# Products that nobody reads, added to TensorE's queue in the first slots of an attention and expert kernel

## Chip, cores and metric

The kernel runs on one core of a Trainium2 chip. The metric is the device time of one execution in microseconds (us). Five engines work side by side, each in its own fixed order: TensorE (PE, with the weight loads PEld beside it), VectorE (DVE), ScalarE (ACT), GpSimd (POOL) and SyncE (SP), from whose queue all DMAs of this kernel are issued.

## What is computed

Eight batches, eight heads, 576 positions, head width 64. First an attention with a bias that is a difference of running sums, then, on its output, a mixture of four attention experts of which two count for each position:

```python
cum = np.cumsum(np.maximum(s, 0.0), axis=-1)
bias = -(cum[:, :, :, None] - cum[:, :, None, :])
scores = np.where(causal, -1e9, q @ k.T / 8 + np.minimum(bias, 0.0))
x = softmax(scores) @ v                       # heads side by side: 512 columns
...
logits = x @ w_gate                           # the best 2 of 4 experts, softmax over the two
y_e = softmax(causal((x @ wq[e]) @ (x @ wk[e]).T / 8)) @ (x @ wv[e]) @ wo[e]
out = sum over the chosen e of weight_e * y_e
```

## The kernel before

The work is cut into pairs of heads (or of experts), numbered n = 0, 1, 2 and so on. Four pairs make a batch of the first attention; the projections (`p...`) and the expert pairs of a batch are mixed into the pairs of the next one. For each pair TensorE makes bf16 products that give bounds for the row maxima (`maxima`, line 482, six banks `m0` to `m5`), VectorE reduces them (`M0` to `M5`, line 496) and joins two columns (`cb`, line 516), TensorE turns the column of maxima (`mt`, line 520), ScalarE copies it with the sign changed (`mA`), and two small DMAs lay it as a row beside q (`mq`, line 529). Then come the scores in fp32r, two products for each piece (lines 547 and 552, steps `s0` to `s6`; the second reads the row of maxima and the running sums), the exponentials on ScalarE (`E0` to `E6`, line 568), masks and column sums on GpSimd (`d0` to `d3`, lines 589 to 614), and the products with v in float32 (`v0` to `v7`, line 645, written to tiles `pvp`). What is lost in rounding q and k is made up by the `l` steps (lines 457 and 462, on VectorE, for pair 1 on GpSimd).

The order of all of it is written out by hand. `slot(n)` gives the named steps of one slot, and FILLING (the first slots), MIDDLE and DRAINING list `slot:step` in the order in which they are issued. A slot prepares ahead: slot n holds the scores of pair n, the products with v of pair n-1, the maxima of pairs n+1 (banks 3, 4, 5) and n+2 (banks 0, 1, 2). So the run begins with slots -2 and -1, where only the maxima of pairs 0 and 1 can be made. Each engine takes its instructions in that order and waits by itself for what they need.

The eight banks of the accumulation memory go round in a list: `take` pops the bank that was given back longest ago, in the order of the text, and `give` puts one at the end. Who takes a bank waits until its last reader is done.

Before the first maxima, VectorE fills constant rows of K2 and Q2 (lines 220 and 221), makes the running sums (lines 281 to 292), and two DMAs bring those of pair 0 to K2 (line 410). `WOH` (the high part of wo) is written by ScalarE from the weights' steps `w0` and `w1` of slot 6.

Of the kernel before, what the change touches and what calls it, by code (L numbers as in the profile page):

```python
# [8 lines left out]
F32 = mybir.dt.float32  # L9
F32R = mybir.dt.float32r  # L10
# [29 lines left out]
def pieces(kt, q0, q1):  # L40
# [4 lines left out]
    for ci, segs in enumerate(SCHUNKS):  # L45
# [59 lines left out]
)  # L105
MIDDLE = {
# [1055 lines left out]
```

## Time and profile before

| | us |
|---|---|
| three timed runs | 678.67, 679.19, 681.6 |
| their median | 679.19 |
| span of the profiled execution, from its first to its last instruction | 682.3 |
| PE busy in it | 652.6 (96%) |
| DVE, ACT, POOL busy in it | 553.7, 453.1, 445.2 |
| mean granted clock of TensorE in it | 0.990 |

The profiled execution has no time of its own beside its span. The span lies 3.1 us above the median of the timed runs and 0.7 above the longest of them. A row of the timeline gives the start and the duration in us, the engine, line and operation, the tiles written and read, the shape, how many instructions are merged in the row, and in brackets how long the engine was idle before it and what ended that. The granted clock of a stretch is 1.00 for 2.4 GHz and 0.50 for 1.2 GHz, and the record of it begins with a row at 44.66 us: a stretch before that reads 1.00 in the windows for want of a record.

### The profile page before, as it was taken

To read this page: it belongs to the slowest core of one execution; us is meant where nothing else is said; L and a number is where in the kernel's file an instruction comes from. 1 tells how busy PE (TensorE), PEld (TensorE's weight loads), DVE (VectorE), ACT (ScalarE), POOL (GpSimd) and SP (SyncE) were. 2 spreads that over 40 slices of the span, in tenths; PEclk is the share of its full clock that TensorE was granted. 3 is DMA by queue.
4 is the path that set the end of the run, shared out by engine and by line. 5 is a ranking of instruction groups with operands and counts; after the bars stand their busy time and mean duration, and the time that the engine had idled before them with its cause. 6 is when DMAs were issued, how large, how long until landed. Compare 5 with 4: busy or idle time off the path is not lost.

```text
span 682.3 us, 16339 instructions
## 1 busy us (share of the span) xinstructions
PE 652.6 (96%) x5816; PEld 537.6 (79%) x5816; DVE 553.7 (81%) x1480; ACT 453.1 (66%) x972; POOL 445.2 (65%) x608
## 2 busy tenths in 40 slices
PE   1898899999999999999999999999999999999997
PEld 1665588878988798878987888878987788889875
DVE  6778988897889878888888878897888988871974
ACT  6567877666667756766767766676667766566464
POOL 8676676675786678576775677766876776837120
PEclk9999999979999999999999999999999999999989
DMA  4435352262347534554436633565346543340413
GB/s 131 113 104 139 115 161 73 74 177 55 107 111 187 163 91 106 154 145 132 120 94 159 183 90 89 148 163 152 95 103 165 161 113 106 86 123 11 99 40 123
DMA packets 52158, 81.21 MB, mean 119 GB/s; under 512 B 18430, under 2 KB 26622, under 8 KB 52078
## 3 DMA queue, kind: packets, MB, share of 16 engines
q1 hardware_dynamic: 52078, 80.18, 43.6%
q8 instruction: 46, 0.75, 0.5%
q14 instruction: 34, 0.28, 0.2%
HBM read 44.55 MB, written 10.09 MB: 80 GB/s over the span
## 4 chain that ended last, share of the span: by engine, by line
PE 83%; DMA 4%; DVE 4%; POOL 3%; SPq 2%; issue 2%; ACT 2%; ACTq 0%; POOLq 0%; DVEq 0%
PE pvp L645 18%; PE pq L855 15%; PE s L547 10%; PE s L552 10%; PE mx L482 9%; PE pw L855 8%; PE po L855 6%; DMA k<-cum 3%; PE sm L696 3%; DVE mx L496 1%; PE mt L520 1%; PE po L829 1%; DMA rb<-rr 1%; POOL r L611 1%; DVE q L457 1%
## 5 line engine op out<-in xcount | busy, mean ns | idle before, releaser
L496 DVE CUSTOM_DVE_ANT_0 mx<-mx,mask 128x512 f32<-128x512 f32 (+5 forms) x480 | 217.2, 471 | 61.4 <-PE mx L482 41.4
L589 POOL TENSOR_SCALAR_AFFINE_SELECT p<-p 128x256 f32<-128x256 f32 (+1 forms) x240 | 122.0, 509 | 148.5 <-ACT p L568 145.2
L568 ACT ACTIVATE p<-s 128x512 f32<-128x512 f32 x288 | 159.6, 588 | 65.4 <-PE s L552 48.2
L547 PE MATMUL s<-q,k 128*128 128x320 f32 (+3 forms) x672 | 175.2, 291 | 4.0 <-DVE k L462 1.6
L552 PE MATMUL s<-q,k 97*128 97x320 f32 (+3 forms) x672 | 163.3, 288 | 1.0 <-DMA q<-mr 1.0
L547 PEld LDWEIGHTS s<-q,k 128*128 128x128 f32 (+1 forms) x672 | 126.7, 189 | 17.6 <-issue 5.8
L611 POOL TENSOR_TENSOR r<-r,p 128x640 f32<-128x640 f32 x92 | 128.9, 1401 | 7.7
L552 PEld LDWEIGHTS s<-q,k 97*128 97x128 f32 (+1 forms) x672 | 126.3, 189 | 3.1 <-DMA q<-mr 1.7
L482 PE MATMUL mx<-k,q 96*64 96x384 bf16 (+6 forms) x960 | 97.8, 307 | 14.1 <-DMA k<-p 11.1
L645 PE MATMUL pvp<-p,v 128*64 128x128 f32 (+4 forms) x1024 | 101.9, 341 | 0.4 <-ACT p L568 0.4
L457 DVE TENSOR_TENSOR q<-raw,q 64x576 fp32r<-64x576 f32 x94 | 84.0, 895 | 14.9 <-ACT q L422 12.4
L645 PEld LDWEIGHTS pvp<-p,v 128*64 128x64 f32 x1024 | 70.5, 139 | 21.2 <-issue 3.1
L462 DVE TENSOR_TENSOR k<-raw,k 64x576 fp32r<-64x576 f32 x94 | 82.3, 888 | 5.0 <-DMA k<-k 3.1
L482 PEld LDWEIGHTS <-q 96*64 96x64 bf16 x960 | 47.6, 114 | 47.3 <-issue 14.5
L855 PE MATMUL pq<-xh,wqkh 128*128 128x288 f32 x256 | 77.7, 303 | 0.0
L855 PE MATMUL pq<-xh,wqkl 128*128 128x288 f32 x256 | 75.5, 295 | 0.0
L855 PE MATMUL pq<-xl,wqkh 128*128 128x288 f32 x256 | 75.4, 294 | 0.0
L425 ACT ACTIVATE k<-raw 64x576 fp32r<-64x576 f32 x96 | 64.5, 681 | 4.0 <-DMA raw<-in_qk_dram 1.7
L496 DVE DVE_READ_ACCUMULATOR2_ANT mcol<- 128x1 f32 x480 | 65.7, 137 | 0.9
L422 ACT ACTIVATE q<-raw 64x576 fp32r<-64x576 f32 x96 | 63.9, 678 | 3.4 <-DMA raw<-in_qk_dram 2.7
L606 POOL TENSOR_TENSOR r<-p 128x256 f32<-128x256 f32 x46 | 40.5, 880 | 35.4 <-ACT p L568 35.4
L659 ACT ACTIVATE pv<-pvp 128x256 f32<-128x256 f32 (+1 forms) x92 | 36.1, 405 | 40.6 <-PE pvp L645 40.6
(120 smaller groups left out, 1172.0 us busy)
## 6 DMA issues: line engine op xcount, KB each, us to landing
raw<-in_qk_dram SPq DMA_DIRECT2D x30, 576.0 KB
rb<-rr SPq DMA_DIRECT2D x92, 144.0 KB
q<-q SPq DMA_DIRECT2D x45, 288.0 KB
k<-k SPq DMA_DIRECT2D x39, 288.0 KB
v<-in_vm_dram SPq DMA_DIRECT2D x32, 256.0 KB
out_dram<-o SPq DMA_DIRECT2D x32, 256.0 KB
q<-mr SPq DMA_DIRECT2D x96, 2.2 KB
raw<-in_qk_dram SPq DMA_DIRECT2D x4, 288.0 KB
```

Source lines behind the costliest of these rows:

```text
L425: nc.scalar.activation(k2[0:64, j], get_raw(n, j)[64:128], AF.Copy)
L457: eng.tensor_tensor(a[64:128, j], get_raw(n, j)[0:64], q2[0:64, j].bitcast(F32), op=OP.subtract)
L462: eng.tensor_tensor(c[0:64, j], get_raw(n, j)[64:128], c[64:128, j].bitcast(F32), op=OP.subtract)
L482: nc.tensor.matmul(t[64 * j : 64 * j + 64, c0 : c0 + k1 - k0], q2[0:RC, 64 * qt : 64 * qt + 64], k2[0:RC, k0:k1], start=True, stop=True,)
L496: nc.vector.tensor_tensor_reduce(t[:, c0 : c0 + w], t[:, c0 : c0 + w], mask[:, m0 : m0 + w], scale=1.0, scalar=NEG, op0=OP.add, op1=OP.max ...
L547: nc.tensor.matmul(t[0:nk, c0 : c0 + q1 - q0], K1[r1(n)][:, j, k0 : k0 + nk], Q1[r1(n)][:, j, q0:q1], start=True, stop=False,)
L552: nc.tensor.matmul(t[0:nk, c0 : c0 + q1 - q0], K2[r2(n)][0 : RM + 1, j, k0 : k0 + nk], Q2[r2(n)][0 : RM + 1, j, q0:q1], start=False, stop= ...
L568: nc.scalar.activation(ptile[n][:, x % 2, 512 * ci : 512 * ci + 512], tl[x], AF.Exp, scale=0.125)
L589: nc.gpsimd.affine_select(out=a, in_=a, pattern=[[0, 2], [1, nk]], compare_op=OP.is_ge, fill=0.0, base=0, channel_multiplier=-1,)
L611: add(r[:, :, q0:S], r[:, :, q0:S], p[:, :, 1024 + c : 1024 + c + S - q0], op=OP.add)
L645: nc.tensor.matmul(cur[h][64 * j : 64 * j + 64, q0 - PVC[h] : q1 - PVC[h]], vsl(j, kt), ptile[n][:, j, c : c + q1 - q0], start=first, stop ...
L855: nc.tensor.matmul(t[0:nk, 0:w], l, r, start=(x == 0), stop=(x == len(terms) - 1))
```

## The change

54 steps named `e`, `er`, `eq` and `ef` are put into FILLING; the order of all other steps stays as it was. Each takes one bank or two, multiplies a constant tile by itself into them on TensorE and gives them back at once. Nobody reads the result. The constant tile is the memory of `WOH`, whose first 256 float32 columns VectorE sets to 1.0, ahead of its other fills; read as bf16 they are 512 columns, every second one zero.

- `e`: one bf16 product, 128 rows by 128 columns of weights, 512 columns streamed.
- `er`: two bf16 products, each on one half of the rows (64 by 128), 512 columns each.
- `eq`: four bf16 products, each on a quarter of the array (64 by 64), 512 columns each.
- `ef`: two fp32r products on the halves of the rows (64 by 128), 256 columns each.

28 of them (13 `e`, 6 `er`, 6 `eq`, 3 `ef`) stand at the very start, 12 `e` after the last maxima of pair 0 are reduced, and 14 `e` at seven places further on.

```diff
 FILLING = (
+    "0:e 0:e 0:e 0:e 0:e 0:e 0:e 0:e 0:e 0:e 0:er 0:er 0:er 0:er 0:er 0:eq 0:eq 0:eq 0:eq 0:eq "
+    "0:ef 0:ef 0:ef 0:e 0:er 0:e 0:eq 0:e -2:h1 -2:h3 -2:h2 -2:h0 -2:hc -1:m5 -2:m1 -1:m4 -2:M1 "
...
+    "-1:lq -2:M0 0:e 0:e 0:e 0:e 0:e 0:e 0:e 0:e 0:e 0:e 0:e 0:e -1:mt -1:h3 0:h1 0:l1 0:l0 -1:hc "
...
+    "0:f2 0:hc 1:ld 0:lq 0:e 1:m5 0:d0 0:m0 0:s6 0:mt 0:E4 0:s5 0:mA 1:lk 1:l0 0:m1 0:m2 0:E2 1:m4 "
+    "0:E5 0:M1 1:h1 1:h3 1:M5 0:M0 0:E6 1:M4 0:e 0:e 1:m3 1:l1 1:lq 1:M3 1:h2 0:mq 1:hc 1:s4 1:s5 "
+    "1:s6 1:s1 1:s2 1:E6 1:E5 1:s3 1:cb 0:M2 1:E2 0:e 0:e 0:e 1:mt 1:w0 1:s0 0:d1 0:lv 0:d2 1:l3 "
+    "2:h2 2:hc 1:E4 1:h0 2:h3 0:e 1:m0 1:v2 1:l2 1:v4 1:v3 1:v5 1:mA 1:E1 1:E3 1:v0 1:E0 2:h0 2:h1 "
...
+    "2:E1 2:E3 3:m5 2:m2 1:V0 2:s5 3:m4 3:lk 1:M2 2:M5 2:cb 2:ld 0:e 2:mt 2:M2 2:mA 2:l1 2:m0 2:a0 "
...
+    "3:m2 3:V0 3:E6 3:s2 3:E2 3:E0 3:M0 3:r4 2:V0 2:V1 3:mq 4:m5 2:d3 0:e 4:v2 3:d0 4:s3 3:n1 3:E5 "
...
+    "4:l1 5:l2 5:w0 3:d3 4:a1 5:h0 4:A1 4:w0 5:h2 4:mq 4:v6 4:E1 4:hc 0:e 0:e 0:e 0:e 0:e 5:m4 "
...
     fill(0)
 
+    idle = const.tile([P, 2, DM], F32R, tag="woh", name="woh")
+    WOH = idle
+    nc.vector.memset(idle[:, 0, 0:256].bitcast(F32), 1.0)
     nc.vector.memset(K2[1][64:96].bitcast(F32), 0.0)
...
+    def spare(kind):
+
+        w = WOH[:, 0, 0:256].bitcast(BF16)
+        a = take("e0")
+        if kind == "e":
+            nc.tensor.matmul(a, w[:, 0:P], w, start=True, stop=True)
+            give(a)
+            return
+        c = take("e1")
+        for r, t in enumerate((a, c)):
+            k = slice(64 * r, 64 * r + 64)
+            if kind == "er":
+                nc.tensor.matmul(t, w[k, 0:P], w[k], start=True, stop=True)
+            elif kind == "ef":
+                nc.tensor.matmul(
+                    t[:, 0:256], WOH[k, 0, 0:P], WOH[k, 0, 0:256], start=True, stop=True
+                )
+            else:
+                for o in (0, 64):
+                    nc.tensor.matmul(t[o : o + 64], w[k, 0:64], w[k], start=True, stop=True)
+        give(a)
+        give(c)
...
     for n, x in order(pairs):
-        if x in steps[n]:
+        if x in ("e", "er", "eq", "ef"):
+            spare(x)
+        elif x in steps[n]:
             steps[n].pop(x)()
```

## Rows read from the trace of the kernel before

**Rows 1.** The page: the engines' busy time and share of the span, and the granted clock in 40 slices of the span (tenths).

```profile
PE 652.6 (96%) x5816; PEld 537.6 (79%) x5816; DVE 553.7 (81%) x1480; ACT 453.1 (66%) x972; POOL 445.2 (65%) x608
...
PEclk9999999979999999999999999999999999999989
```

**Rows 2.** Windows of the whole program: stretch, its length, busy time (and instructions) of PE, PEld, DVE, ACT and POOL, granted clock, share of the DMA engines, GB/s.

```profile
44.70:82.20 37.50, 32.87 (x303) 21.50 (x299) 34.04 (x88) 28.82 (x59) 25.36 (x34) 1.00 0.48 135
82.21:85.61 3.40, 3.40 (x20) 2.18 (x18) 3.16 (x14) 3.11 (x7) 3.15 (x7) 0.50 0.29 83
...
143.65:150.40 6.75, 6.63 (x44) 5.01 (x45) 5.66 (x13) 3.48 (x9) 4.39 (x7) 0.50 0.44 86
...
659.10:662.40 3.30, 3.30 (x22) 2.08 (x20) 2.48 (x4) 1.67 (x5) 1.52 (x5) 0.50 0.29 98
```

**Rows 3.** Timeline of PE: neighbouring score products in three stretches (the first of each two streams 320 columns, and the next starts when those have gone in), and two products of 512 columns near the end. The row at 25.65 holds two banks of maxima, each two products of 512 columns on the two halves of the array's columns.

```profile
22.16 0.47 PE L552 MATMUL s<-q,k 97*128 97x320 f32 x1
22.43 0.36 PE L547 MATMUL s<-q,k 128*128 128x192 f32 x1
...
25.65 1.06 PE L482 MATMUL mx<-k,q 96*64 96x512 bf16 x4
...
45.60 0.31 PE L552 MATMUL s<-q,k 97*128 97x320 f32 x1
45.75 0.25 PE L547 MATMUL s<-q,k 128*128 128x192 f32 x1
...
82.66 0.47 PE L552 MATMUL s<-q,k 97*128 97x320 f32 x1
82.93 0.36 PE L547 MATMUL s<-q,k 128*128 128x192 f32 x1
...
671.28 0.39 PE L829 MATMUL po<-woh,xh 128*128 128x512 f32 x1
671.51 0.39 PE L829 MATMUL po<-wol,xh 128*128 128x512 f32 x1
```

**Rows 4.** Windows of the first 60 us, columns as in rows 2: from the first reduction to the first score, the scores of pairs 0 and 1, the first products with v, and what follows.

```profile
12.45:21.60 9.15, 3.62 (x29) 1.96 (x25) 8.89 (x25) 4.12 (x7) 8.73 (x21) 1.00 0.27 78
21.76:37.90 16.14, 16.07 (x77) 12.98 (x77) 12.37 (x42) 8.60 (x17) 10.97 (x17) 1.00 0.46 132
37.90:44.66 6.76, 6.07 (x33) 3.68 (x35) 3.23 (x8) 5.39 (x11) 2.92 (x6) 1.00 0.34 83
44.66:60.00 15.34, 14.12 (x137) 9.92 (x133) 14.61 (x47) 11.49 (x23) 13.84 (x19) 1.00 0.42 118
```

**Rows 5.** Timeline of PE: the first maxima, the turn of pair 0, the maxima of pair 1, the first score, the first unbroken run of products with v, two later waits of PE, and the later of the products with v of pair 1.

```profile
10.69 0.37 PE L482 MATMUL mx<-k,q 96*64 96x256 bf16 x1 [10.69 <-DMA k<-p]
11.46 2.56 PE L482 MATMUL mx<-k,q 96*64 96x256 bf16 x19 [0.39 <-DMA k<-p]
18.10 0.37 PE L520 MATMUL mt<-ident,mcol 128*9 128x128 f32 x1 [4.08 <-DVE mcol L496]
18.40 1.76 PE L482 MATMUL mx<-k,q 96*64 96x320 bf16 x16
21.76 0.61 PE L547 MATMUL s<-q,k 128*128 128x320 f32 x1 [1.60 <-DVE k L462]
...
38.59 0.37 PE L520 MATMUL mt<-ident,mcol 128*9 128x128 f32 x1 [0.76 <-DVE mcol L496]
...
40.20 4.29 PE L645 MATMUL pvp<-p,v 128*64 128x320 f32 x20
...
51.27 0.56 PE L482 MATMUL mx<-k,q 96*64 96x256 bf16 x8 [0.54 <-DVE mcol L496]
...
55.13 1.68 PE L645 MATMUL pvp<-p,v 128*64 128x192 f32 x16
...
80.06 0.64 PE L482 MATMUL mx<-k,q 96*64 96x512 bf16 x4 [1.85 <-DMA k<-cum]
```

**Rows 6.** Timeline of DVE: two fills, the first reduction, the last of pair 0 and the last step ahead of the first score, and the three reductions at which it waited for PE.

```profile
1.11 1.02 DVE L220 MEMSET k<- 32x1152 f32 x1 [1.11 <-PEq L1150]
...
3.39 0.11 DVE L228 MEMSET ones<- 128x64 f32 x1
...
12.47 0.57 DVE L496 CUSTOM_DVE_ANT_0 mx<-mx,mask 128x384 f32<-128x384 f32 x1 [3.93 <-PE mx L482]
...
17.66 0.23 DVE L496 CUSTOM_DVE_ANT_0 mx<-mx,mask 128x64 f32<-128x64 f32 x1
...
20.86 0.75 DVE L462 TENSOR_TENSOR k<-raw,k 64x576 fp32r<-64x576 f32 x1
...
26.34 0.70 DVE L496 CUSTOM_DVE_ANT_0 mx<-mx,mask 128x512 f32<-128x512 f32 x1 [2.06 <-PE mx L482]
...
31.05 0.57 DVE L496 CUSTOM_DVE_ANT_0 mx<-mx,mask 128x384 f32<-128x384 f32 x1 [1.26 <-PE mx L482]
...
44.91 0.57 DVE L496 CUSTOM_DVE_ANT_0 mx<-mx,mask 128x384 f32<-128x384 f32 x1 [3.70 <-PE mx L482]
```

**Rows 7.** Timeline of POOL: where it begins on the masks and sums of pairs 0 and 1 after a wait, and its last step for pair 1.

```profile
26.98 0.41 POOL L589 TENSOR_SCALAR_AFFINE_SELECT p<-p 128x256 f32<-128x256 f32 x1 [3.80 <-ACT p L568]
...
42.02 0.73 POOL L606 TENSOR_TENSOR r<-p 128x256 f32<-128x256 f32 x1 [3.75 <-ACT p L568]
...
50.52 0.45 POOL L614 TENSOR_TENSOR r<-r,p 64x128 f32<-64x128 f32 x1
```

**Rows 8.** Timeline of SP, DMA issues: the running sums of pair 0 and its row of maxima (two DMAs each).

```profile
8.64 1.58 SPq L410 DMA_DIRECT2D k<-p  x2
...
18.80 1.53 SPq L529 DMA_DIRECT2D q<-mr  x2
```

More of the change, by code (lines that the diff above doesn't have):

```diff
@@ L242, in tile_attention_then_moe @@
     WVGL = const.tile([P, NC, 260], F32R, tag="wvgl", name="wvgl")
-    WOH = const.tile([P, 2, DM], F32R, tag="woh", name="woh")
     WOL = const.tile([P, 2, DM], F32R, tag="wol", name="wol")
```

72 rows, old and new, of the table FILLING are left out of this document.

## The prediction

> **What bounds the kernel now.** I read the page's first lines, then windows, then the engines' timelines of the first 60 us. On the page PE is busy for 96% of the span, and the granted clock is 90% or more in all but two of its 40 slices [rows 1]. That leaves nothing for added products to win, unless they change the clock, so the reader should look at where the clock is low. Of the windows from 44.70 us on, three read 0.50, in all 13.5 us: 82.21 to 85.61, 143.65 to 150.40, 659.10 to 662.40 [rows 2]. What the page hides is the start. No row tells the clock before 44.66; it has to be read from the products. A score product of 320 columns takes 0.27 us till the next starts at 22.16, and 0.15 at 45.60; in the stretch that is granted 0.50, at 82.66, it takes 0.27 again [rows 3]. So TensorE runs at 1.2 GHz from its first product to about 44.7 and at 2.4 after that.
>
> Who sets the pace in those 44.7 us? Three parts [rows 4]. Up to 21.6 it is VectorE: busy 8.89 of 9.15 us from its first reduction, at 12.47, to its last step ahead of the first score [rows 4, 6]; PE waits 4.08 us in there for the last maxima of pair 0 [rows 5]. From 21.76 to 37.90 it is PE: busy 16.07 of 16.14. From 37.90 to 44.66 again PE, with 6.07 of 6.76, most of it one run of products with v, 40.20 to 44.49 [rows 4, 5]. VectorE waits for PE's maxima in these two parts three times: 2.06, 1.26 and 3.70 us, 7.0 together [rows 6]; POOL waits 3.80 and 3.75 us for exponentials, which wait for scores [rows 7]. From 44.66 to 60 VectorE is busy 14.61 of 15.34 [rows 4]: a faster PE helps there only by what reaches it earlier.
>
> **The first 28 steps.** They remove nothing. The constant tile costs VectorE one fill ahead of its others: 256 columns, by the fill of 1152 in 1.02 us and that of 64 in 0.11 [rows 6] about 0.28 us. It pushes the two fills behind it, the running sums and so the DMA issued at 8.64 [rows 8], which the first maxima await (10.69 and 11.46, [rows 5]): +0.3 us there. The products can start at about 1.5. A product of 512 columns takes 0.23 us at the high level [rows 3] and by the 0.27 for 320 columns 0.43 at the low one. At the low level: 13 `e` 5.6 us; `er` and `eq` 12 x 0.43 = 5.2 if the parts of the array work beside each other; 3 `ef` 0.6. Sum 11.4. If the row halves go one after the other, 5.2 + 0.6 more, 17.2. That column halves go together is in the row at 25.65: four products of 512 columns in 1.06 us [rows 3]; of row halves the trace of before has none. I take 11.4, the nearest row.
>
> The Trainium skill, "TensorEngine Tiling (Array Packing)", section "Tiling Modes", says that tiles work independently and that row halves are such tiles. By it the sum is 11.4; no run here shows it.
>
> If the level rises half way, at about 6, the products end near 6 + (11.4 - 4.5)/2 = 9.5, inside PE's wait for the DMA (to 10.69), and cost nothing. If it never rises they end at 12.9, and the first maxima come up to 1.4 late; with 17.2 and a rise at 6 they end at 12.4, 0.7 after the second DMA with its 0.3. That is the price if the cover is gone.
>
> Does the level rise? What PE did before each rise: before 44.66 an unbroken run of float32 products with v on both column halves, all 128 rows [rows 5]. What did not raise it: 16 us of scores and maxima with PE busy throughout [rows 4], half of which fill 97 rows or 96 by 64. So being busy is not enough here, and the added products, all rows and all columns back to back, are nearer to the run that raised it than to the scores that didn't.
>
> The Trainium skill, "TensorE: Matmul & The Clock Gate", Part 1, has the low clock as the default that matmul activity lifts. By that alone the scores should have lifted it well before 44.66; the trace disagrees, with its 16.07 busy us at 0.27 per 320 columns.
>
> **The 12 steps after the last maxima of pair 0.** Each takes the oldest bank. Two are free at once, four come free as the reductions go on, so the products spread over PE's wait of 4.08 us. The sixth bank's reduction is the last, at 17.66 to 17.95 [rows 6]; behind it stand five products and only then the turn `mt`: 5 x 0.23 = 1.2 us at the high level, 2.2 at the low. Queued behind: `mt` (18.10), the copy, two DMAs (18.80), the maxima of pair 1 (18.40) [rows 5, 8]. VectorE reads the latter only after 21.6, so they have room. The row of maxima is needed at 22.16; its second DMA is issued at some 19.6 and, if it takes the 2.05 us from 8.64 to 10.69 [rows 5, 8], lands at 21.6: 0.5 to spare. The reductions gain some 0.3 from a faster first bank. So the first scores start 0 to 1.6 us later; I take 0.3.
>
> **What the high level gives from 21.76 on.** PE's work there halves, but the saving counts only until something else is late. On VectorE's side the three waits are the ceiling, 7.0 us. First wait: the four score banks ahead of the reduced one take 21.76 to 25.65 at the low level, 2 less at the high one: 1.8 of 2.06 comes back. Second: 0.9 of 1.26, since VectorE itself comes to it earlier. Third: the products with v go from 4.29 to 2.15: 2.1 of 3.70. Together 4.8. On POOL's side, its start moves with the exponentials and it works without a break from 42.02 to 50.97; if it starts 3.2 earlier it ends pair 1 at 47.8, and the later products with v of pair 1, at 55.13 before [rows 5, 7], would need it by 55.13 - 4.8 = 50.3. So POOL does not take it away; VectorE, busy 95% after 44.66 [rows 4], is next.
>
> **The other 14.** Six stand ahead of 40 us, in PE's waits for VectorE that a faster PE makes longer (0.76 at 38.59 already, [rows 5]): nothing at the high level. One follows just before the products with v, hidden by the same. Two in slot 2 and the end of slot 3 have no wait of their own in the rows: 2 x 0.23 = 0.5. The five in slot 4, 1.2 us, lie in the wait of 1.85 us for the running sums, from 78.2 to 80.06 [rows 5]. In the profiled execution the clock falls at 82.2 soon after that wait, and PE, all busy, loses half of 3.4 us, 1.7 [rows 2]. If the five prevent it, 0 to 1.7 comes back; the timed runs are 0.7 to 3.6 shorter than the profiled span, so I take 0.4, near the low end. The ring of banks: each added step hands the next real product a bank freed later. Bounds 0 and, for a few of them, the 0.54 that PE waits for a reduction at 51.27 [rows 5]: I take 0.3.
>
> **Sum.** -4.8 + 0.3 + 0.5 + 0.3 - 0.4 = -4.1 (the fill's 0.3 is within the later start). The timed runs carry no profile, so I set it against the median: 679.2 - 4.1 = 675.1. After 60 us each slot waits for the one before, so I let it reach the end whole.
>
> **Rivals.**
> *It falls back before the scores* (0.27). Between 13 and 21.7 PE has only the 12 products and 1.8 us of maxima; the falls in the profile came behind waits of PE (1.85 us before the fall at 82.2). If TensorE is at 1.2 GHz when the first score starts, the scores run as before, and every `e` stands in a PE that is busy throughout: seven at 0.43 less the 0.76 of wait is 2.2, the start is up to 1.6 late, the fill 0.3: +4.1, less up to 2.1 if the extra products bring the rise forward. 681.2 to 683.3, I say 682.1, slower. For it: the spread of the products, those 16 us that didn't lift the clock. Against: at the low level each `e` lasts twice as long and fills more of the wait. The point that decides is the spacing of the first scores.
> *Caught by another engine* (0.17). The level is high, but POOL or the DMAs for pairs 1 and 2 hold: only the first wait and a part of the second come back, 2.5, less 1.1: 677.5 to 678.
> *The constant tile doesn't lift the clock at all* (0.08): 12.9 to 18.7 for the end of the first 28, 1.5 to 7 late, and 2 to 4 for the others: 683 to 690.
> *More comes back* (0.05): all 7.0 of the waits and the 1.7: 671.
>
> **Chances and range.** The forecast, 672.5 to 676.8, has 0.43. Half a per cent, 3.4 us, is about what a measurement of this kernel can tell from no change: faster below 675.8, slower above 682.6. Faster: three quarters of the forecast and the last rival, 0.37. Slower: a quarter of the fall back and most of the dead tile, 0.14. The rest, 0.49, is within. The range takes in the forecast, the catch and most of the fall back: 672.0 to 682.5, with 0.15 or so outside.
>
> **What would show it.** Right: score products of 320 columns 0.15 apart at 22, VectorE's three waits shorter, the products with v of pair 0 over by about 39, the same row of pair 1 near 51, a first maxima no later than 11.5. Wrong: 0.27 apart at 22 with `e` products 0.43 apart between them; a first maxima after 12; the high level at 22 but POOL or a DMA as the releaser of the next slots.

## The result, and the profile after

| | us |
|---|---|
| after, median of 20 runs | 682.42 (675.87 to 686.88) |
| before, median of 20 runs on the same chip | 678.33 (674.71 to 682.54) |
| ratio, 95% interval | 1.0054, 1.0031 to 1.0078 |
| profiled execution of after: its time, its span | 683.88, 682.2 |

The change costs half a per cent, where the prediction had a gain of 4.1 us. The time lies at the upper end of the range, 0.1 under its bound, and at 682.1 a rival had been set; that rival's mechanism is not what happened, as the rows show. The ratio leaves out one slow execution of after (686.88), so it is not the quotient of the two medians.

The page of after: busy time of the engines, and the granted clock in 40 slices of the span.

```profile
PE 661.3 (97%) x5897; PEld 536.5 (79%) x5897; DVE 549.9 (81%) x1481; ACT 453.1 (66%) x972; POOL 450.1 (66%) x608
...
PEclk9889899999999999999999999999999999999999
```

Beside [rows 1] PE is 8.7 us longer busy, and the low slices now stand in the first 90 us. Windows of after, columns as in rows 2, cut where the granted clock changes:

```profile
6.59:16.82 10.23, 8.12 (x70) 3.28 (x67) 6.42 (x22) 6.51 (x11) 8.52 (x21) 1.00 0.31 93
16.83:20.23 3.40, 2.98 (x12) 1.13 (x13) 3.29 (x7) 1.36 (x4) 3.35 (x4) 0.50 0.00 0
20.24:30.47 10.23, 6.54 (x56) 4.63 (x52) 6.20 (x23) 3.76 (x8) 4.59 (x8) 1.00 0.60 161
30.48:40.71 10.23, 9.91 (x44) 6.95 (x44) 8.75 (x25) 7.24 (x15) 7.44 (x10) 0.50 0.18 59
...
81.68:88.50 6.82, 6.82 (x45) 4.76 (x45) 4.25 (x17) 4.77 (x9) 5.80 (x9) 0.50 0.50 140
```

So TensorE reaches 2.4 GHz at 6.59, falls to 1.2 at 16.83, is up again at 20.24, falls at 30.48 for 10.2 us and once more at 81.68. In the third row PE is busy only 6.54 of 10.23 us. The timeline of PE, with the rows that answer rows 3 and 5, says why (line 340 is `e`, 347 `er`, 354 `eq`, 349 `ef`; 509 the maxima, 547 the turn, 574 and 579 the scores, 672 the products with v):

```profile
1.26 4.45 PE L340 MATMUL e<-woh 128*128 128x512 bf16 x10 [1.26 <-DVE woh L224]
5.64 1.70 PE L347 MATMUL e<-woh 64*128 64x512 bf16 x10
7.27 1.27 PE L354 MATMUL e<-woh 64*64 64x512 bf16 x20
...
10.79 0.27 PE L509 MATMUL mx<-k,q 96*64 96x256 bf16 x1
11.46 1.45 PE L509 MATMUL mx<-k,q 96*64 96x256 bf16 x19 [0.40 <-DMA k<-p]
...
17.25 2.29 PE L340 MATMUL e<-woh 128*128 128x512 bf16 x5 [0.53 <-DVE mcol L523]
19.34 0.42 PE L547 MATMUL mt<-ident,mcol 128*9 128x128 f32 x1
...
21.95 0.41 PE L579 MATMUL s<-q,k 97*128 97x320 f32 x1 [0.57 <-DMA q<-mr]
...
23.32 0.31 PE L579 MATMUL s<-q,k 97*128 97x320 f32 x1
23.47 0.26 PE L574 MATMUL s<-q,k 128*128 128x192 f32 x1
...
29.03 0.56 PE L509 MATMUL mx<-k,q 96*64 96x256 bf16 x8 [3.01 <-DMA k<-cum]
...
29.77 0.28 PE L547 MATMUL mt<-ident,mcol 128*9 128x128 f32 x1
...
32.29 1.08 PE L340 MATMUL e<-woh 128*128 128x512 bf16 x2 [0.32 <-ACT p L595]
...
34.30 0.47 PE L579 MATMUL s<-q,k 97*128 97x320 f32 x1
34.56 0.36 PE L574 MATMUL s<-q,k 128*128 128x192 f32 x1
...
40.45 0.41 PE L547 MATMUL mt<-ident,mcol 128*9 128x128 f32 x1
...
41.77 2.24 PE L672 MATMUL pvp<-p,v 128*64 128x320 f32 x20
...
80.36 0.59 PE L340 MATMUL e<-woh 128*128 128x512 bf16 x2 [1.59 <-ACT p L595]
```

Four things are to be seen. The first maxima are where they were (10.79 and 11.46, against 10.69 and 11.46 in [rows 5]), so the prefix is hidden. The score product of 320 columns at 23.32 is followed after 0.15 us: the first scores do run at the high level, as forecast. Then stands a wait of 3.01 us for `k<-cum` that rows 5 do not have there: it is the load of pair 2's running sums. And the scores of pair 1 behind it are 0.26 us apart again (34.30), with two `e` ahead of them that last 1.08 us together.

Why are the sums late? The DMA issues of SP in after:

```profile
20.09 1.53 SPq L556 DMA_DIRECT2D q<-mr  x2
21.66 0.52 SPq L1138 DMA_DIRECT2D cum<-p  x1
...
25.62 0.28 SPq L440 DMA_DIRECT2D k<-cum  x1
```

In before, the issues of SP that follow the row of maxima of [rows 8] by one place and by three:

```profile
20.37 0.52 SPq L1111 DMA_DIRECT2D cum<-p  x1
...
24.34 0.28 SPq L413 DMA_DIRECT2D k<-cum  x1
```

SP issues in order. The row of maxima (`mq`) waits for the turn, 1.24 us later than before; behind `mq` stands the store of the running sums of all pairs to memory (`-1:cu`, line 1138), and behind that the load of pair 2's part (`0:hc`, line 440), which must wait until the store has landed. Everything slides by 1.3 us. The chain of work of after in this stretch (start, duration, what; the longest pieces) goes through exactly these:

```profile
17.25 2.29 PE e L340 x5
...
20.09 0.78 SPq L556
20.91 0.71 SPq L556
21.66 3.89 DMA cum<-p
25.62 3.28 DMA k<-cum
...
29.03 0.56 PE mx L509 x8
```

This stretch of it begins with the five `e` behind the last reduction. The same maxima in before:

```profile
27.85 0.90 PE L482 MATMUL mx<-k,q 96*64 96x256 bf16 x8
```

There a PE at the low level came to them at 27.85 without a wait; the sums, issued at 24.34, were there at about 27.6 if the load took the same 3.28 us (an estimate). A PE at the high level gets there at 26.0 and stands. On VectorE (timeline, the waits that answer rows 6):

```profile
24.72 0.70 DVE L523 CUSTOM_DVE_ANT_0 mx<-mx,mask 128x512 f32<-128x512 f32 x1 [1.22 <-PE mx L509]
...
29.80 0.75 DVE L484 TENSOR_TENSOR q<-raw,q 64x576 fp32r<-64x576 f32 x1 [2.64 <-PE s L574]
31.16 0.57 DVE L523 CUSTOM_DVE_ANT_0 mx<-mx,mask 128x384 f32<-128x384 f32 x1 [0.61 <-PE mx L509]
...
44.29 0.57 DVE L523 CUSTOM_DVE_ANT_0 mx<-mx,mask 128x384 f32<-128x384 f32 x1 [1.80 <-PE mx L509]
```

The three waits of rows 6 shrank from 7.02 to 3.63 us together, and a new one of 2.64 us took most of that.

### The profile page after: what moved, and what is told of

Same layout as the page of the kernel before. It is cut to its first block, busy times and chain, and to the rows that moved or that the text cites. A ratio compares the mean times of both kernels' runs of the same rounds, so it can differ in the third digit from the quotient of the medians.

```text
span 682.2 us, 16497 instructions
## 1 busy us (share of the span) xinstructions
PE 661.3 (97%) x5897; PEld 536.5 (79%) x5897; DVE 549.9 (81%) x1481; ACT 453.1 (66%) x972; POOL 450.1 (66%) x608
## 4 chain that ended last, share of the span: by engine, by line
PE 82%; DMA 6%; DVE 4%; ACT 3%; issue 2%; SPq 1%; POOL 1%; ACTq 0%; DVEq 0%; POOLq 0%
PE pvp L672 16%; PE pq L882 15%; PE s L574 10%; PE s L579 10%; PE mx L509 9%; PE pw L882 8%; PE po L882 7%; PE sm L723 3%; DVE mx L523 2%; DMA k<-cum 2%; DMA rb<-rr 1%; DMA q<-mr 1%; PE mt L547 1%; PE po L856 1%; ACT p L595 1%
## 5 line engine op out<-in xcount | busy, mean ns | idle before, releaser
L616 POOL TENSOR_SCALAR_AFFINE_SELECT p<-p 128x256 f32<-128x256 f32 (+1 forms) x240 | 124.4, 519 | 145.1 <-ACT p L595 141.0
L574 PE MATMUL s<-q,k 128*128 128x320 f32 (+3 forms) x672 | 172.8, 287 | 1.2 <-ACT k L452 0.7
L579 PE MATMUL s<-q,k 97*128 97x320 f32 (+3 forms) x672 | 161.3, 285 | 2.2 <-DMA q<-mr 2.2
L574 PEld LDWEIGHTS s<-q,k 128*128 128x128 f32 (+1 forms) x672 | 124.9, 186 | 14.2 <-issue 4.5
L579 PEld LDWEIGHTS s<-q,k 97*128 97x128 f32 (+1 forms) x672 | 124.0, 186 | 4.9 <-DMA q<-mr 3.4
L509 PE MATMUL mx<-k,q 96*64 96x384 bf16 (+6 forms) x960 | 95.2, 301 | 6.0 <-DMA k<-cum 4.8
L672 PE MATMUL pvp<-p,v 128*64 128x128 f32 (+4 forms) x1024 | 100.0, 336 | 0.1
L509 PEld LDWEIGHTS <-q 96*64 96x64 bf16 x960 | 46.0, 112 | 40.1 <-issue 15.9
```

What stands on the lines that cost most here:

```text
L509: nc.tensor.matmul(t[64 * j : 64 * j + 64, c0 : c0 + k1 - k0], q2[0:RC, 64 * qt : 64 * qt + 64], k2[0:RC, k0:k1], start=True, stop=True,)
L574: nc.tensor.matmul(t[0:nk, c0 : c0 + q1 - q0], K1[r1(n)][:, j, k0 : k0 + nk], Q1[r1(n)][:, j, q0:q1], start=True, stop=False,)
L579: nc.tensor.matmul(t[0:nk, c0 : c0 + q1 - q0], K2[r2(n)][0 : RM + 1, j, k0 : k0 + nk], Q2[r2(n)][0 : RM + 1, j, q0:q1], start=False, stop= ...
L616: nc.gpsimd.affine_select(out=a, in_=a, pattern=[[0, 2], [1, nk]], compare_op=OP.is_ge, fill=0.0, base=0, channel_multiplier=-1,)
L672: nc.tensor.matmul(cur[h][64 * j : 64 * j + 64, q0 - PVC[h] : q1 - PVC[h]], vsl(j, kt), ptile[n][:, j, c : c + q1 - q0], start=first, stop ...
```

## Experiments

Theories, by letter: A, the five products behind the last reduction hold the turn, and with it SP's queue with the store and the load of the sums; PE waits, and the clock falls behind that wait. B, the later products cost PE their own time, or the waits for banks. C, the first 28 (or their fill) delay the start. D, only how often the clock falls back in an execution counts, not the change. Ratios are to the kernel before, on the same chip in the same session, with 95% intervals. Diffs are against the changed kernel, most of them as what became of the lists of steps. A rise or fall is that of the one profiled execution.

**Parts alone.** The first 28 with the fill; the 12 without the others; the 14 without the others (each with the fill).

```diff
 only28:  the list keeps its first two lines
-"-1:lq -2:M0 0:e (x12) -1:mt"   and the 14
+"-1:lq -2:M0 -1:mt"
 only12:  keeps "0:e (x12)" alone;   only14:  keeps the 14 alone
```

> The constant tile and the first 28 steps alone; the 12 and the 14 are left out. Theory A (the five products behind the last reduction hold the turn of pair 0, and with it the store of the running sums that stands behind it in SP's queue): the turn is at 18.0 to 18.4, the load of the sums of pair 2 is issued near 24.3 as before, no 3 us wait of PE for it; the time is that of before, 676.5 to 679.5. Theory B (each later product costs PE its own time, where the clock is low or where it waits for a bank; the start plays no part): the time is that of before too, 677.5 to 679.5. Theory C (the first 28 and the fill themselves delay the start): first maxima over 0.5 us later than 10.69 and 11.46, and 680 or more.

> The constant tile and the 12 steps behind the last reduction of pair 0 alone. TensorE is then at 1.2 GHz when they run, unless they lift it. Theory A: the turn of pair 0 comes 2 us later than at 18.10, the store of the sums and the load behind it as well; 679.5 to 682. Theory B: 12 x 0.43 mostly in PE's wait, 678.5 to 680. Theory C: 678 to 679.

> The constant tile and the 14 later steps alone. Theory A: the turn of pair 0 at 18.1 as before, the time 678 to 680. Theory B: the seven ahead of 42 us cost 2 us at the low level, the five in slot 4 wait for banks that ScalarE holds and push the maxima behind them by 1 us: 681 to 683. Theory C: 678 to 679.

only28: 1.0012 (0.9984 to 1.0039). The first maxima come at 10.81 and 11.49, no wait for the sums, the turn at 17.39. The clock rises at 4.3 and falls at 14.5 until 24.8. So the 28 cost nothing that can be seen, and without the 12 the level is gone before the scores: C falls. only12: 1.0034 (1.0013 to 1.0055), the turn at 18.67, and the wait for the sums is there without the prefix: 2.79 us before 27.78, the clock low from 27.2. only14: 1.0017 (0.9986 to 1.0048), the clock rises at 37.1. Of the three parts only the 12 have an interval that lies above 1, as A says; the three intervals overlap.

**The store of the sums ahead of the row of maxima.** All 54 steps stay; only SP's order changes.

```diff
-"-1:lq -2:M0 0:e ..."   "... -1:m1 -1:cu 0:h2"
+"-1:cu -1:lq -2:M0 0:e ..."   "... -1:m1 0:h2"
```

> The changed kernel with one DMA moved: the store of the running sums (line 1138) stands ahead of the 12 steps in SP's queue and no longer behind the row of maxima of pair 0. Theory A: the store is issued near 14, the load of pair 2's sums no later than 24, PE's wait of 3.0 us at 26 goes and the scores of pair 1 start near 31 and not at 33.9; 678 to 680.5, 2 to 4 below the changed kernel. Theory B: the wait goes, the time stays within 1.5 of 682.4. Theory C: as theory B.

1.0003 (0.9977 to 1.003): the half per cent is gone. The store is issued at 12.15 instead of 21.66. But the load still goes out at 23.05, since a load of raw q and k (`0:ld`) stands ahead of it, and PE waits 2.18 us. Its clock falls at 26.3, for 10.2 us. From the issues of SP and the timeline of PE in cu_early:

```profile
23.05 0.29 SPq L440 DMA_DIRECT2D k<-cum  x1
...
27.24 0.90 PE L509 MATMUL mx<-k,q 96*64 96x256 bf16 x8 [2.18 <-DMA k<-cum]
```

So a part of A's chain is cut, not all. Two things follow. The load goes out 1.3 us earlier here than in before (24.34), and a PE at the high level waits for it all the same: the held turn is only a part of the wait of after, the earlier PE is the other. And the time is level although the wait and the fall behind it are still in this profile, which speaks against A as the whole of the half per cent.

**Fewer behind the last reduction, and the five of slot 4.** e12to7 keeps 7 of the 12, so none is left behind the last reduction; no_hc5 leaves out the five of slot 4.

```diff
 e12to7:
-"-1:lq -2:M0 0:e (x12) -1:mt"
+"-1:lq -2:M0 0:e (x7) -1:mt"
 no_hc5:
-"4:E1 4:hc 0:e 0:e 0:e 0:e 0:e 5:m4"
+"4:E1 4:hc 5:m4"
```

> The changed kernel with 7 of the 12 steps behind the last reduction of pair 0, so that none waits for the last bank. Theory A (five products behind the last reduction hold the turn and SP's queue behind it): the turn at 17.4 and not at 19.3, the load of pair 2's sums issued near 23.8 and not at 25.6, PE's wait of 3.0 us 1 to 2 shorter; time 678 to 680.5. Theory B (the later 14 cost, not the 12): within 1.5 of 682.4. Theory D (it is only how often the clock falls back, whatever the turn does): fewer products in the wait let it fall more often, 682 to 684.

> The changed kernel without the five steps in slot 4. They took five banks in the order of the ring and waited 1.59 us for ScalarE with the maxima of pair 6 behind them. Theory A: within 1 of 682.4, or 681.4 at the least. Theory B: those maxima start no later than the sums' load allows, 679.5 to 681.4. Theory D: a wait of PE is open again, 682 to 684.

e12to7: 1.0041 (1.0014 to 1.0069), the turn at 18.20, the wait for the sums 0.31 us, and the clock is low from 19.06 to 25.9, in the first scores. The chain of A is nearly gone and the ratio is hardly better than that of after, which speaks against A. That the five not only hold the turn but also keep TensorE up would explain it; it is not shown. no_hc5: 1.0097 (1.0065 to 1.013; six runs). The wait of 3.14 us is there, and the clock falls at 81.39 for 6.8 us as it does with the five. For these five B falls: in this profile they neither bring nor prevent that fall.

**The bank of an added step given back to the head of the list**, so that the next real product gets the bank that it had before the change.

```diff
+    def back(t):
+        banks.insert(0, taken.pop(id(t))[1])
-            give(a)
+            back(a)
...
-        give(a)
-        give(c)
+        back(c)
+        back(a)
```

> The changed kernel, but the banks of the added steps go back to the head of the ring, so that each added product takes the bank that the next real one takes and none waits for a reduction on its own account. Theory A: the 12 run in one go from 13 to 15.8, the turn is at 17.4, the five in slot 4 end before the sums' load lands: 677 to 680. Theory B: the bank waits go, the products' own time stays: 679.5 to 681.5. Theory D: PE then stands still from 15.8 to 17.4 and from 18.5 to 21; the clock falls back at the same rate, 681 to 683.

1.024 (1.0208 to 1.0272; six runs), the clearest slowdown of all. Each added product now goes into the bank of the one before. Timeline of PE:

```profile
1.26 6.37 PE L343 MATMUL e<-woh 128*128 128x512 bf16 x10 [1.26 <-DVE woh L224]
...
19.48 2.61 PE L512 MATMUL mx<-k,q 96*64 96x256 bf16 x20
...
22.69 6.98 PE L343 MATMUL e<-woh 128*128 128x512 bf16 x11 [0.60 <-PE mx L512]
```

Ten products take 6.37 us instead of 4.45, the first maxima come at 19.48, and the clock rises only at 56.0. This turned out to be another experiment than the one meant: what the ring of banks costs in the changed kernel stays open. It is not what slows it, for cu_ld, below, has the ring of after and is level with the kernel before.

**Both moves on SP, with and without the added products.** The load of the sums (`0:hc`) also goes ahead of the raw load. cu_ld has all 54 steps, none_ld none of them (the fill stays).

```diff
-"-1:lq -2:M0 ..."   "... -1:m1 -1:cu 0:h2"   "0:s0 0:ld 0:E0"   "0:f2 0:hc 1:ld"
+"-1:cu -1:lq -2:M0 ..."   "... -1:m1 0:h2"   "0:s0 0:E0"   "0:f2 0:hc 0:ld 1:ld"
```

> No added product: the kernel before with the constant tile's fill and two moves in SP's queue, the store of the running sums ahead of the row of maxima of pair 0 and the load of raw data of pair 3 behind the load of pair 2's sums. It tells what these moves are worth by themselves. Theory A: PE did not wait for that load in the kernel before, so 677.5 to 679.5, no change. Theories B and D: the same.

> The changed kernel, all 54 steps, with both moves in SP's queue: the store of the running sums early, and the raw data of pair 3 behind the load of pair 2's sums. Theory A: that load is issued near 21 and PE does not wait for it (3.0 us in the changed kernel); ratio to the kernel before 0.995 to 1.001. Theory D (the clock falls back in PE's other waits as often as before): 1.003 to 1.006, as the changed kernel.

none_ld: 1.0033 (1.0005 to 1.0061); its profile runs much like that of before, with the turns of pairs 0, 1 and 2 each 0.2 us later. The moves alone bring nothing. cu_ld: 1.0002 (0.997 to 1.0033), median 677.2 against 677.98. Its profiled execution is the closest to that of after, for its clock runs like that of after up to 30.5 us: up at 6.65, down at 16.89, up at 20.30. Windows of cu_ld, columns as in rows 2:

```profile
20.30:30.47 10.17, 8.10 (x68) 5.30 (x64) 8.58 (x32) 6.24 (x12) 6.46 (x10) 1.00 0.37 119
30.48:40.71 10.23, 8.85 (x71) 6.03 (x70) 9.28 (x25) 8.88 (x18) 8.43 (x11) 1.00 0.36 96
```

Timeline of PE in cu_ld:

```profile
19.43 0.42 PE L547 MATMUL mt<-ident,mcol 128*9 128x128 f32 x1
...
26.05 0.57 PE L509 MATMUL mx<-k,q 96*64 96x256 bf16 x8
...
27.31 0.28 PE L547 MATMUL mt<-ident,mcol 128*9 128x128 f32 x1 [0.34 <-DVE mcol L523]
...
35.04 0.28 PE L547 MATMUL mt<-ident,mcol 128*9 128x128 f32 x1 [0.33 <-DVE mcol L523]
...
36.60 2.25 PE L672 MATMUL pvp<-p,v 128*64 128x320 f32 x20
```

DMA issues of SP in cu_ld:

```profile
12.15 0.50 SPq L1138 DMA_DIRECT2D cum<-p  x1
...
20.18 1.53 SPq L556 DMA_DIRECT2D q<-mr  x2
21.83 0.38 SPq L440 DMA_DIRECT2D k<-cum  x1
```

The maxima of pair 2 start at 26.05 without a wait, PE is busy 8.10 us instead of 6.54 up to 30.47, and the clock stays at 1.00. The turns of pairs 0, 1 and 2 are at 19.34, 29.77 and 40.45 in after and at 19.43, 27.31 and 35.04 here. So the wait costs 2.5 us by pair 1, and the low stretch behind it another 2.9 by pair 2: 5.4 us in all. The spans are 682.2 and 674.3.

**What of the rest is needed.** With both moves: the 28 and the 12 without the 14 (a28_12_ld); the 28, 7 of the 12 and seven of the 14 (e7_ld); and the 28 with products that take a bank which is free at once instead of the oldest (hold).

```diff
 a28_12_ld: cu_ld without the 14
 e7_ld: cu_ld with "0:e (x7) -1:mt", of the 14 only those ahead of 42 us
 hold: 28, then added steps of kinds h and k
+        if kind == "h":
+            banks.insert(0, banks.pop(-2))
+        if kind == "k":
+            banks.insert(0, banks.pop(1))
...
+        if kind == "k":
+            nc.tensor.matmul(a, w[:, 0:P], w, start=True, stop=True)
+            banks.insert(0, taken.pop(id(a))[1])
+            return
```

> The first 28, the 12, both moves; none of the 14 later ones. Theory A: as cu_ld or up to 0.003 lower, since the later ones cost PE time at the low level. Theory D: without them the clock falls back from 26 to 40 us and does not rise before the products with v: 1.002 to 1.006.

> The first 28, seven of the 12, the seven steps ahead of 42 us, both moves; without the seven steps of slots 2 to 4. Theory A: nothing holds the turn or the sums, 0.994 to 1.000. Theory D: the wait from 13 to 21 is thinner filled than in the changed kernel, the clock falls more often there, 1.001 to 1.005.

> The first 28, both moves, and other fillers after them, so placed that none waits for a bank that a real product doesn't wait for and none stands behind the last reduction: two for each reduction of pair 0 but the last, five between the maxima of pair 1 and the first scores, and twelve at five of the changed kernel's places. If the clock then stays at 2.4 GHz from 8 to 60 us, it tells what that is worth. Theory A and D both: fewer low stretches before 45 us than the changed kernel's four, the scores of pair 2 (45.4 in the kernel before) start 4 to 6 earlier, ratio 0.992 to 0.998. If the clock holds and the time is still 1.000 or more, the gain is lost behind 60 us, and both theories fall.

a28_12_ld: 1.0002 (0.9981 to 1.0023), so the 14 bring nothing that can be measured. e7_ld: 1.0025 (1.0003 to 1.0047). No wait for the sums, but after its fall the clock stays down, as in this window:

```profile
16.70:40.50 23.80, 21.62 (x103) 15.00 (x103) 18.74 (x56) 13.30 (x26) 16.04 (x26) 0.50 0.24 77
```

With the five behind the last reduction the same fall was over at 19.9 to 21.1 (after and its third execution, no_hc5, cu_ld, a28_12_ld). Here the prediction's rival of a fall before the scores is to be seen as it was described. hold: 1.0029 (1.0005 to 1.0053), the clock high from 6.8 to 30.7 and low until 37.5, with no DMA waited for there; PE's longest wait ahead of that fall is 1.42 us for ScalarE, up to 29.78. So A's wait is not the only thing behind which the clock falls near 30 us.

**Further executions of the same kernels**, one profiled execution each, for what varies by itself; nothing of the kernels is changed.

> The changed kernel once more, another execution. Theory A: a wait of PE of 2 to 3.5 us for the load of pair 2's sums at 26 to 30 whenever the clock is high then, and the clock falls within 5 us of it. Theory D: falls at other waits, not at this one.

> The changed kernel a third time; theories A and D expect the same of it as of the second look.

> The changed kernel with both moves, another execution. Theory A: no wait of over 0.5 us for that load. If the clock is high from 21 to 45, the scores of pair 2 start 4 to 6 us earlier than at 45.4; if it falls back between 13 and 21 and stays low, 0 to 1 earlier. Theory D: the latter is the common case.

> The kernel before, another execution. Its first low stretch should end between 37 and 46 us, with the products with v of pair 0, and its falls behind that at the same waits (78, 140) or none: a span of 673 to 682.

> The kernel before, a third execution. Either a first rise of the clock between 20 and 36 us, during the scores of pairs 0 and 1, with the scores of pair 2 starting 3 to 6 us ahead of 45.4; or one between 37 and 46, with the products with v, and those scores at 45 to 46.

> The kernel before, a fourth execution; either case as in the third look, a rise between 20 and 36 us or one between 37 and 46 us.

| execution | time | clock rises | turn of pair 2 | wait for the sums of pair 2 | low near 30 us |
|---|---|---|---|---|---|
| after, 2, 3 | 683.88, 684.99, 681.64 | 6.6, 5.5, 4.1 | 40.45, 39.39, 40.33 | 3.01, 2.59, 2.59 | from 30.5, 29.3, 28.0; 10.2 to 13.7 long |
| cu_ld, 2 | 676.1, 672.96 | 6.7, 5.5 | 35.04, 33.83 | none | none |
| before | none of its own | 44.7 | 38.59 | none | low from the start |
| before 2, 3, 4 | 677.48, 677.94, 678.96 | 24.5, 41.2, 36.8 | 35.53, 38.09, 38.17 | 0.53, none, 0.52 | none; low; low |

The wait and the fall behind it are in each profile of after. But the kernel before lifts its clock by itself, and at very different times. Its second execution, timeline of PE:

```profile
24.37 0.35 PE L547 MATMUL s<-q,k 128*128 128x256 f32 x1
...
26.83 0.56 PE L482 MATMUL mx<-k,q 96*64 96x256 bf16 x8 [0.53 <-DMA k<-cum]
```

Its fourth:

```profile
27.45 0.90 PE L482 MATMUL mx<-k,q 96*64 96x256 bf16 x8 [0.52 <-DMA k<-cum]
```

In the second the rise came in the middle of the first scores, and PE waited 0.53 us for the sums of pair 2, with a turn at 17.68. The fourth, low until 36.8, waits 0.52 us there as well. So this wait does not tell the levels apart; it shows that the load has next to no slack in the kernel before, added products or not. In the three executions of after the turn is 1.1 to 1.7 us later and the clock high from 21.1 or earlier, and the wait is 2.6 to 3.0 us.

Over all profiles in which the clock was up at 25 us: with a wait of 2 us or more for the sums (after three times, no_hc5, only12, cu_early) it fell in or behind that wait, between 26 and 30.5, in six of six and stayed low 10 us or longer; without one (cu_ld twice, only28, before_look2, a28_12_ld, hold) in two of six, for 6.8 us.

## Why the prediction was wrong

**The first 28: right.** The level rose at 6.6 against "at about 6", the products end at 10.7 and not "near 9.5", just inside their cover, the first maxima are not late (10.79 and 11.46), and the row halves run beside each other: ten products of 512 columns in 1.63 us (5.64 to 7.27) are 0.33 a pair, while one after the other they would take 0.46 at the high level alone. The fill's 0.3 us did not show: the DMA of the sums of pair 0 is issued at 8.64 as in [rows 8]. The rule of the Trainium skill, "TensorEngine Tiling (Array Packing)", section "Tiling Modes", agrees with this row.

**The premise of the low start: one execution taken for the kernel.** "So TensorE runs at 1.2 GHz from its first product to about 44.7" was true of the profile [rows 3]. Three more executions of the same kernel rose at 24.5, 41.2 and 36.8, two of them inside scores; "being busy is not enough here" held for the one execution. Their turns of pair 2 come 0.4 to 3.1 us earlier than 38.59 [rows 5]. That much of the 4.8 us was there to be had without the change. It could have been suspected: the profiled span lay above all three timed runs. The profile of after has nearly the same span, 682.2 against 682.3, so this pair does not show what the medians lost. Beside the other executions of the table it can be seen: the turn of pair 2 comes at 40.1 on average in the three of after and at 37.6 in the four of before. Of the 4.0 us between their mean spans 2.5 have come by then; where the other 1.5 are lost was not followed.

**The 12 steps: the failed step.** The prediction let the five behind the last reduction hold the turn, and priced that by the row of maxima alone, with 0.5 us to spare. That term was right in size: the first score product with the row comes at 21.95, against 22.16 [rows 3]. But its list of what is queued behind named "the copy, two DMAs (18.80), the maxima of pair 1" and stopped there. Two further issues on SP follow, the store of the sums and the load through it, 3.89 and 3.28 us to landing in the chain of after. The sum had no term for them; PE waits 3.01 us there. Their slack was what the low clock had given PE, the very thing that the change takes away: of the 3.01 us the later turn is 1.3 (the load goes out at 25.62, not 24.34), the rest is a PE that is there at 26.0 and not at 27.85. cu_early and cu_ld, which change only the order in SP's queue, are level with the kernel before (1.0003 and 1.0002, where after has 1.0054), and the same moves alone gain nothing (1.0033). And the five took 2.09 us, not 1.2, because the clock fell at 16.83 among the spread ones.

**What the high level gives: the size was near, in a kernel without that wait.** VectorE's three waits gave back 3.4 of the 4.8 us in after; the new wait took 2.64. In cu_ld the products with v of pair 0 start at 36.60, 3.6 us earlier than in [rows 5], and VectorE is 5.8 us ahead of the profile of before at 45 us. Neither POOL nor another engine took that away up to there, as the prediction argued (the longest waits of PE behind the first score are 0.93 us for ScalarE and 0.89 for a DMA). But the second execution of before is as far without any added product: its turn of pair 2 is at 35.53, that of cu_ld at 35.04.

**"I let it reach the end whole": wrong.** The clock falls again later, in a number and length that differ between executions. From the mean granted clock of each timed run, (1 - clock) x 2 x span is its time at the low level behind the first rise: in cu_ld's twelve runs 4.0 to 31.3 us, with times of 672.8 to 682.8, and 0.34 us of time for each us at the low level (fitted, correlation 0.92). In after it is 20.5 us on average against 16.0 in cu_ld. (For the kernel before the sum can't be made, since the low start is not in its record.) Of cu_ld's lead at 45 us its median keeps 0.8 us, which the interval does not tell from nothing; a part of that lead was only the late rise in the one profile of before.

**The five of slot 4: not what they were given for.** The 0.4 us stood for preventing a fall at 82. The fall is there (81.68, 6.8 us long against 3.4 in [rows 2]), without the five as well, and PE waits 1.59 us for a bank in the middle of them. The 3.4 was again one execution: in the other three of before the fall near 76 to 79 us lasts 6.8. Over the six runs of no_hc5 the time at the low level, worked out as above, is 30.4 us on average against 20.5 in after, so the five may prevent other falls; that was not followed.

**The rival that met the time.** "It falls back before the scores" gave 682.1, and 682.4 was measured. Its deciding point, the spacing of the first scores, went against it: 0.15 at 23.32. The clock did fall before the scores, at 16.83, but was up again at 20.24; the fall that cost time came at 30.48, behind a wait for a DMA that no rival named. The second rival, a DMA that holds PE, had the nearer mechanism and too low a price, because it left the clock up behind the wait. The Trainium skill, "TensorE: Matmul & The Clock Gate", Part 1, section "HAM oscillation — how this bites in real kernels", describes a PE that waits for a DMA and comes back at the low clock. The trace agrees in part: behind the wait of 3.01 us TensorE comes back at the high level at 29.03, and falls 1.45 us later.

**What stays open.** Whether any part of the change is a gain: cu_ld and a28_12_ld are level with the kernel before, no version beats it. none_ld at 1.0033, with a trace hardly different from before, warns that a ratio of 0.3% says little here; e12to7, hold and e7_ld are not ranked by theirs. Why the clock fell at 30 us in a28_12_ld and hold and not in cu_ld was not found. D is not refuted: within a kernel the time follows the time at the low level (0.34 us for each us in cu_ld), and A only names one wait that goes with such a fall. And that the wait causes the fall is shown by counts (six of six against two of six) and by one pair of like executions, not by a run that changes the wait alone at a fixed clock.

## What to carry to other kernels

When a step that issues DMAs is held up, follow its queue past the first transfer: the one that breaks may be the third, and its slack is to be counted at the speed that the faster engine will have. A wait that a faster TensorE newly meets can cost twice: here 2.5 us for itself and 2.9 for the low stretch behind it. Before building on the clock of one profile, look at several executions: the same kernel rose at 24.5 in one and at 44.7 in another.

## What the runs showed of the hardware that was not expected

- Products of 512 columns that follow each other into one bank take 0.64 us each at the low level (6.37 for ten), and 0.44 when each goes into another bank (4.45 for ten). In ring_head, which goes the first way, TensorE was busy 51.3 of the 54.9 us up to 55.9 and its clock rose only at 56.0; in after it rose at 6.6.
- The first rise of the clock varies by 20 us between executions of one kernel without added products (24.5 to 44.7), and only by 2.6 us with them (4.1 to 6.7 in after and cu_ld).
- A store to memory and the load of it back took 3.89 and 3.28 us in the chain of after, 7.2 us together. The store is 432 KB, the sums of all pairs; the load is 13.5 KB, those of one pair.
